# A decode step of two attention layers: VectorE takes seven of eight value chunks and also adds key blocks

## The chip, the core and the metric

The kernel runs on one NeuronCore of a Trainium2 chip. The metric is the device time of one execution in microseconds (us). Every input lies in the chip's main memory in float32 and is streamed into the on-chip memory (SBUF, 128 partitions) while TensorE (PE), VectorE (DVE), ScalarE (ACT) and GpSimd (POOL) compute. SyncE (SP) issues the loads. All of them read instructions in order, each from its own list, and wait for one another by semaphores.

## The reference

One token passes twice through the same attention layer A and the same MLP layer B. The cache of keys and values has 32 heads of 4096 positions of 128 numbers.

```python
def _A_ref(x, k_cache, v_cache, wq, wo):
    B, Sq, D = x.shape                                     # 1, 1, 512
    H, Dh = 32, 128
    q = (x @ wq).reshape(B, Sq, H, Dh).transpose(0, 2, 1, 3)
    scores = jnp.einsum("bhqd,bhkd->bhqk", q, k_cache) * (Dh ** -0.5)
    p = _softmax(scores, axis=-1)
    o = jnp.einsum("bhqk,bhkd->bhqd", p, v_cache)
    return o.transpose(0, 2, 1, 3).reshape(B, Sq, H * Dh) @ wo

def _B_ref(x, w1, b1, w2, b2):
    h = _gelu(jnp.einsum("bsd,df->bsf", x, w1) + b1)       # F = 1376
    return jnp.einsum("bsf,fd->bsd", h, w2) + b2

x = A_x
x = x + _A_ref(_layernorm(x, axis=-1), A_k_cache, A_v_cache, A_wq, A_wo)
x = x + _B_ref(_layernorm(x, axis=-1), B_w1, B_b1, B_w2, B_b2)
x = x + _A_ref(_layernorm(x, axis=-1), A_k_cache, A_v_cache, A_wq, A_wo)
x = x + _B_ref(_layernorm(x, axis=-1), B_w1, B_b1, B_w2, B_b2)
```

Keys and values together are far larger than SBUF, so each layer reads them again, apart from a little that is kept at the change of layers.

## The kernel before

**Tiles.** The 32 heads form G = 8 groups of J = 4. A group has one block K and one block V, each 128 partitions by 16,384 numbers, in C = 8 chunks of 2048 (NC). A chunk of V holds, for each of the four heads, 512 positions: 128 on the partitions, times four key blocks of 128 numbers each (U = 512 numbers per head). A third load of a group, the pair, brings the group's part of `wo` and the next group's part of `wq` (2 x 2048 numbers).

**Homes.** K and V go around three homes of one large tile, `arena`: A, B and C (`RING`). K of the group after next lies where V of this group lay. The pair has one home, `PAIR`. `SCRATCH`, `TURNED` and the rest have places behind them.

**Order of the loads.** All loads are issued by SP in the order of the program: K, V, pair, K, V, pair. A load waits until its home's last reader is done, and every later load waits behind it. Line 108 issues them all.

**One group.** `group` computes the scores, chunk by chunk into the PSUM tile `pS` (`scores`, four narrow products side by side, one per head). Between chunks it finishes the group before (`ahead`). Behind chunk 4 (`SUM_BEHIND`) `sum_up` adds what VectorE has made into the PSUM tile `pO`, and `head` (line 286 on) turns `pO`, picks out the blocks on the diagonal, and sums the four key blocks. Behind chunk 6 `out_product` multiplies with `wo`, and so frees the pair. Then come chunk 7, the softmax (`exponentials`, lines 230 to 239) and the turned weights (`weights`, lines 244 to 253). In the last group of layer two the output product stands behind chunk 7 instead.

**Values.** `partly` gives the first `by_pe` chunks of V to PE (`values`), which writes four rows per head, one per key block, of which the diagonal is wanted. `weighted` (line 264) multiplies the other chunks in place by the softmax weights, in one VectorE instruction over the whole remainder. Then `next_queries` forms the next group's queries on PE and VectorE, and `added` sums those chunks on VectorE by halves until one chunk is left. With `by_pe` = 2 there are six chunks: adds of three, one and one chunk. The sum over the 128 partitions is left to `sum_up`: four products of a column of ones with the chunk, one per head.

This way go groups 0 to 5 of layer one, and five groups of layer two, the first of them with `by_pe` = 3. The last two groups of layer one and the first two of layer two give all values to PE, around the change of layers.

**The end.** The last K comes in two halves, the last V in four pieces. Behind them come the last `wo`, `w1` and `w2`, which the MLP takes as they land.

**Order by hand.** `tc.keep_in_program_order` keeps PE's products, the loads, and the multiplications and adds of line 264 in the order in which the program names them. In the trace, products of every helper have line 112, and loads line 108.

Of the kernel before, what the change touches and what calls it, by code (L numbers as in the profile page):

```python
# [14 lines left out]
ALU = mybir.AluOpType  # L15
AX = mybir.AxisListType

P = 128
# [3 lines left out]
G = 8  # L22
J = 4
C = 8
# [4 lines left out]
U = 512  # L29
NC = 4 * U  # L30
# [9 lines left out]
SHARED = B_AT + KEPT_V  # L40
SCRATCH = SHARED + 10 * U
PAIR = SHARED + 11 * U
KEPT_K = PAIR + 2 * NC
TURNED = SHARED + 9 * U
ARENA = KEPT_K + 2 * U
HALVES = ((0, 4), (4, 8))
BY_PE, BY_PE_AT_BEGIN = 2, 3
SUM_BEHIND = 4
ZQ = C - 1 + J * C
WIDE = 32 * J + 8 + 3 + 1  # L50
FRONT = 192
# [8 lines left out]
def decode_layers(ctx: ExitStack, tc: tile.TileContext, vectors, k, v, w, w1, w2, out):  # L60
    nc = tc.nc
# [3 lines left out]
    def ctile(name, *shape):  # L65
        return const.tile([P, *shape], F32, name=name)
# [4 lines left out]
    front = ctile("front", FRONT)  # L71
    arena = const.tile([P, ARENA], F32, name="arena")
    cells = ctile("cells", CELLS)
# [9 lines left out]
    def small(name, n=1):  # L83
        nonlocal first_front, rest
        if name.startswith("gelu_"):
            i = "huaztg".index(name[-1])
            return cells[:, gelu + FB * i : gelu + FB * (i + 1)]
        if name not in places:
            fit = [j for j in range(J) if gaps[j] + n <= ends[j]]
            if name == "by_dma":  # L90
                places[name] = front, first_front, n
                first_front += n
            elif fit:
                places[name] = cells, gaps[fit[0]], n
                gaps[fit[0]] += n
            else:
                places[name] = cells, rest, n
                rest += n
        t, a, m = places[name]
        assert m == n and first_front <= FRONT and rest <= CELLS  # L100
        return t[:, a : a + n]

    def at(first, n):
        return arena[:, first : first + n]
# [6 lines left out]
    def matmul(*a, **kw):  # L111
        tc.keep_in_program_order(nc.tensor.matmul(*a, **kw))  # L112

    def quarters(first):
        return [at(first + U * j, U) for j in range(4)]
# [21 lines left out]
    power = small("power")  # L137
    nc.gpsimd.memset(power, -0.5)

    one = small("one")  # L140
    nc.vector.memset(one, 1.0)


    pS, pO = (psum.tile([P, 512], F32, name=n) for n in ("pS", "pO"))
# [7 lines left out]

    turned_at = [at(TURNED, P)]

# [6 lines left out]
    def pairs(t):  # L161
        return t[:, :8].rearrange("p (c i) -> p c i", i=2)
# [61 lines left out]
    def scores(z, c, kt):  # L224
        for j in range(J):
            matmul(pS[32 * j : 32 * j + C, :], z[:, C * j + C - 1 - c : C * j + 2 * C - 1 - c], kt[j],
                   start=(c == 0), stop=(c == C - 1))

    def exponentials(sc, nsc, between=None):
        nc.vector.tensor_reduce(ml[:, 0:1], pS, axis=AX.X, op=ALU.max)  # L230
        m, bias = small("m"), mt
        nc.vector.transpose(mt, ml)
        nc.vector.tensor_reduce(m, mt[:, :C], axis=AX.X, op=ALU.max)
        nc.vector.tensor_scalar(mb[:, :C], m.to_broadcast([P, C]), nsc, None, op0=ALU.mult)  # L234
        nc.vector.transpose(bias, mb)  # L235
        if between:
            between()
        p = at(SCRATCH, U)
        nc.scalar.activation(p, pS, AF.Exp, bias=bias[:, 0:1], scale=sc, accum_out=ml[:, 0:1])  # L239
        return p  # L240
# [12 lines left out]
        nc.vector.reciprocal(rl, lr[:, 0:1])  # L253
        return pt, rl

    def values(i, pt, vt, c):
        for j in range(J):
            matmul(pO[32 * j : 32 * j + 4, :], pt[:, c, j, :], vt[j],
                   start=(i == 0), stop=(i == C - 1))


# [1 line left out]
    def pinned(*a, **kw):  # L263
        tc.keep_in_program_order(nc.vector.tensor_tensor(*a, **kw))  # L264
# [6 lines left out]
    def added(home, by_pe=BY_PE):  # L271
        first, n = home + NC * by_pe, C - by_pe
        while n > 1:
            m = n // 2
            a, b = at(first + NC * (n - 2 * m), NC * m), at(first + NC * (n - m), NC * m)
            pinned(a, a, b, op=ALU.add)
            n -= m
        return quarters(first)

    def sum_up(t):  # L280
        for j in range(J):
            matmul(pO[32 * j : 32 * j + 4, :], one.to_broadcast([P, 4]), t[j], start=False, stop=True)

    def head(rl, last=False):
        ot = at(SCRATCH, U)
        nc.vector.transpose(ot, pO)  # L286
        o, on = small("o", 4), on_wide
        own = at(SCRATCH, 4 * 129).rearrange("p (b q) -> p b q", q=129)[:, :, :P]
        own = own.rearrange("p b (d q) -> p d b q", q=32)[:, :, :, 0]
        nc.vector.tensor_reduce(o, own, axis=AX.X, op=ALU.add)  # L290
        if last:
            nc.vector.tensor_scalar(on[:, :4], o, rl, None, op0=ALU.mult)  # L292
        else:
            nc.vector.tensor_scalar(in_quarters(on, 4), o.unsqueeze(1).to_broadcast([P, J, 4]), rl, None,
                                    op0=ALU.mult)
        return on
# [7 lines left out]
    def out_product(on, wt, to, narrow=False):  # L304
        for d in range(4):
            if narrow:
                for j in range(J):
                    matmul(to[32 * j : 32 * j + 1, :P], on[:, d : d + 1], wt[:, d, P * j : P * (j + 1)],
                           start=(d == 0), stop=(d == 3))
            else:  # L310
                matmul(to, on[:, d : d + P], wt[:, d, :], start=(d == 0), stop=(d == 3))
# [84 lines left out]
        return t  # L396


    def group(z, acc, ahead, k_blocks, out_behind=C - 2):
        for c, t in k_blocks:  # L400
            scores(z, c, t)
            if ahead and c == SUM_BEHIND:
                t, rl, wt = ahead
                sum_up(t)
                on = head(rl)
            if ahead and c == out_behind:
                out_product(on, wt, pO)
        p = exponentials(sc, nsc)
        if ahead:
            acc = add_up(acc, of_32(turned(pO, wide=True), 4))  # L410
        return acc, *weights(p)

    def partly(pt, v_blocks, home, by_pe=BY_PE):
        for c, t in v_blocks:
            if c < by_pe:
                values(c, pt, t, c)
        weighted(pt, home, by_pe)


    negm, z, sc, nsc = first_queries(xs, s, wq_t, wide=True)  # L420
    acc = pairs(xs)[:, :, 0]
    ahead = None
    for g in range(G):
        final = g == G - 1
        k_home, v_home = RING[2 * g % 3], RING[(2 * g + 1) % 3]
        acc, pt, rl = group(z, acc, ahead, blocks(k, g, k_home, HALVES if final else ((0, C),)))
        ahead = None
        if g == G - 2:
            nc.scalar.copy(at(KEPT_K, 2 * U), at(k_home + NC * C - 2 * U, 2 * U))
        if g < G - 2:  # L430
            partly(pt, blocks(v, g, v_home), v_home)
            pair = load(PAIR, of_w(g % 2, g, 2))
            z = next_queries(xs, negm, by_four(pair[:, NC:]), to=pS)
            ahead = added(v_home), rl, by_four(pair[:, :NC])
            continue
        for c, t in blocks(v, g, v_home, LAST if final else ((0, C),)):
# [3 lines left out]
            if g == G - 2:  # L440
                for j in range(J):
                    i = 4 * c + j - KEPT_V // U
# [8 lines left out]
        else:  # L451
            pair = load(PAIR, of_w(g % 2, g, 2))
            acc = add_up(acc, head_out(rl, by_four(pair[:, :NC])))
            wq_t = by_four(pair[:, NC:])
            z = next_queries(xs, negm, wq_t)
# [26 lines left out]
    negm, z, sc, nsc = first_queries(xs, s, wq_t)  # L482
    make_identity(nc, ident)
    acc = pairs(xs)[:, :, 0]
# [13 lines left out]
    p = exponentials(sc, nsc, lambda: queries(pO, negm, to=at(C_AT + 21 * U, P)))  # L498
    pt, rl = weights(p)
# [3 lines left out]
    acc = add_up(acc, of_32(turned(pO), 4))  # L503

    v_t = [at(B_AT + U * i, U) for i in range(KEPT_V // U)]
    for i, first in enumerate([SHARED, SHARED + U] + [PAIR + U * j for j in range(4)]):
        t = at(first, U)
# [4 lines left out]
    pt, rl = weights(exponentials(sc, nsc))  # L512
    for c in range(C):
        values(c, pt, v_t[4 * c : 4 * c + 4], c)
    acc = add_up(acc, head_out(rl, by_four(pair[:, NC:])))
    z = next_queries(xs, negm, by_four(pair[:, :NC]))

    turned_at[0] = at(TURNED, P)
    homes, ahead = (A_AT, C_AT, B_AT), None
    for n in range(2, G):  # L520
        g, final = G - 1 - n, n == G - 1
        k_home, v_home = homes[(2 * n - 1) % 3], homes[2 * n % 3]
        acc, pt, rl = group(z, acc, ahead, blocks(k, g, k_home, HALVES if final else ((0, C),)),
                            C - 1 if final else C - 2)
        if not final:
            by_pe = BY_PE_AT_BEGIN if n == 2 else BY_PE
            partly(pt, blocks(v, g, v_home, ((0, 6), (6, 8)) if n == 2 else ((0, C),)), v_home, by_pe)
            pair = load(PAIR, of_w(g % 2, g - 1, 2))
            z = next_queries(xs, negm, by_four(pair[:, :NC]), to=pS)
            ahead = added(v_home, by_pe), rl, by_four(pair[:, NC:])  # L530
            continue
        for c, t in blocks(v, g, v_home, LAST):
            values(c, pt, t, c)
            if c in (5, 7):
                idle(pS)
        wo_t = by_four(load(PAIR, of_w(g % 2, g, 1)))
        for a, b in W1_AT_END:
            load_w1(A_AT, a, b)
        for a, b in W2_AT_END:
            load_w2(A_AT + 11 * U, a, b)  # L540
        own = head_out(rl, wo_t, last=True)
# [46 lines left out]
```

## Time and profile before

| what | value |
|---|---|
| median of 3 runs | 673.24 us (672.96 to 673.5) |
| span of the profiled execution | 670.3 us |
| read from main memory | 285.62 MB, 426 GB/s over the span |
| mean granted clock of TensorE | 0.793 |
| matmuls of the scores (K chunks) | 145.2 us busy, 174.9 idle before, most of it for K |
| values on PE (pO from arena) | 81.7 us busy |
| VectorE, line 264 | 260.7 us busy |

The span goes from the first instruction to the last; the timed run holds some 3 us more around it. A row of the timeline gives start, duration, engine, line, operation and tiles, how many instructions were merged, and in square brackets the idle time before it and who ended it. A row of the windows gives for each engine its busy time and number of instructions, then the granted TensorE clock, the DMA share and the rate in GB/s. SPq is SyncE issuing a load.

### The profile page before, as it was taken

How to read it: one execution, taken by the hardware profiler on the slowest of the kernel's cores; microseconds unless marked ns; L12 is line 12 of the kernel's file. 1: busy time of each engine (PE TensorE's matmuls, PEld its weight loads, DVE VectorE, ACT ScalarE, POOL GpSimd, SP SyncE). 2: the span in 40 equal slices, each digit the busy share in tenths (PEclk: the TensorE clock that was granted, in tenths of full speed). 3: DMA queues.
4: the chain of work that ended last, by engine and by line, in shares of the span. 5: the costliest groups of instructions: out<-in, count | busy, mean ns of one | idle time of the engine just before them, and what ended most of it. 6: DMA issues, size and time to landing. Idle time of an engine off the chain costs nothing. (4 is left out here: it accounts for less than half of the span.)

```text
span 670.3 us, 5537 instructions
## 1 busy us (share of the span) xinstructions
PE 384.4 (57%) x2342; PEld 109.2 (16%) x2342; DVE 372.6 (56%) x480; ACT 22.8 (3%) x48; POOL 4.8 (1%) x23
## 2 busy tenths in 40 slices
PE   3533842636618546286768878737617456074586
PEld 1101210101102101021214222111102112011122
DVE  2059388395793965932112221392893966938822
ACT  0010000000000000002000110000000000000000
POOL 1000000000000000000000000000000000000000
PEclk9567785877678658778979998977669868687789
DMA  9999999999999999999999999999999999999996
GB/s 376 438 439 438 434 438 438 405 464 435 438 430 408 430 438 439 438 438 421 426 416 402 431 452 423 437 440 431 426 434 416 457 439 438 435 423 407 438 420 286
DMA packets 11256, 285.97 MB, mean 427 GB/s; under 512 B 1504, under 2 KB 1504, under 8 KB 3296
## 3 DMA queue, kind: packets, MB, share of 16 engines
q1 hardware_dynamic: 11088, 285.61, 99.1%
q8 instruction: 18, 0.29, 0.2%
q14 instruction: 6, 0.05, 0.0%
q10 hardware_dynamic: 144, 0.01, 0.0%
HBM read 285.62 MB, written 0.00 MB: 426 GB/s over the span
## 5 line engine op out<-in xcount | busy, mean ns | idle before, releaser
L264 DVE TENSOR_TENSOR arena<-arena 128x2048 f32<-128x2048 f32 (+4 forms) x44 | 260.7, 5924 | 16.6 <-DMA arena<-in_v 15.9
L112 PE MATMUL pS<-arena,front 128*8 128x512 f32 x1036 | 152.0, 713 | 174.9 <-DMA arena<-in_k 164.5
L112 PE MATMUL pO<-arena 128*4 128x512 f32 x504 | 81.7, 800 | 26.1 <-DMA arena<-in_v 24.5
L112 PE MATMUL pO<-arena,cells 128*128 128x512 f32 (+4 forms) x376 | 82.7, 506 | 17.2 <-POOL cells L186 6.7
L112 PEld LDWEIGHTS pS<-arena,front 128*8 128x8 f32 x1036 | 30.6, 102 | 289.1 <-DVE arena L264 141.9
L286 DVE STREAM_TRANSPOSE arena<-pO 128x512 f32<-128x512 f32 x16 | 11.5, 717 | 110.1 <-PE pO L112 110.1
L112 PE MATMUL pS<-arena,cells 128*1 128x128 f32 (+1 forms) x328 | 55.8, 385 | 18.5 <-DMA arena<-in_w 15.8
L170 DVE STREAM_TRANSPOSE arena<-pO 32x128 f32<-32x128 f32 x64 | 20.0, 312 | 59.0 <-PE pO L112 58.4
L112 PEld LDWEIGHTS pO<-arena,cells 128*128 128x128 f32 (+3 forms) x376 | 28.7, 122 | 64.7 <-issue 35.8
L230 DVE TENSOR_REDUCE cells<-pS 128x1 f32<-128x512 f32 x16 | 11.1, 692 | 50.1 <-PE pS L112 49.8
L244 PE MATMUL pO<-front,arena 128*128 128x128 f32 x64 | 12.0, 318 | 46.2 <-ACT arena L239 46.2
L112 PEld LDWEIGHTS pS<-arena,cells 128*1 128x1 f32 (+1 forms) x328 | 23.9, 120 | 61.2 <-issue 52.8
L239 ACT ACTIVATE arena<-pS,cells 128x512 f32<-128x512 f32 x16 | 12.4, 777 | 507.1 <-DVE cells L235 507.1
L112 PEld LDWEIGHTS pO<-arena 128*4 128x4 f32 x504 | 13.5, 99 | 76.2 <-issue 66.3
L244 PEld LDWEIGHTS pO<-front,arena 128*128 128x128 f32 x64 | 7.6, 154 | 60.2 <-ACT arena L239 59.1
L170 DVE STREAM_TRANSPOSE arena<-pS 32x128 f32<-32x128 f32 x44 | 13.7, 312 | 1.6
L249 DVE STREAM_TRANSPOSE cells<-cells 128x32 f32<-128x32 f32 x16 | 3.4, 214 | 15.9 <-ACT arena L239 15.7
L390 DVE MEMSET pS<- 128x512 f32 x11 | 5.3, 485 | 1.2
L174 DVE STREAM_TRANSPOSE arena<-pS 128x128 f32<-128x128 f32 x3 | 1.0, 317 | 8.9 <-PE pS L112 8.9
L199 DVE TENSOR_SCALAR cells<-cells,pS 128x4 f32<-128x4 f32 x4 | 0.9, 234 | 7.9 <-PE pS L112 7.9
L112 PE MATMUL pO<-arena,front 128*128 128x128 f32 (+2 forms) x18 | 5.1, 382 | 0.0
L247 DVE COPY arena<-pO 128x128 f32<-128x128 f32 x16 | 4.2, 261 | 0.7 <-PE pO L244 0.5
(62 smaller groups left out, 72.5 us busy)
## 6 DMA issues: line engine op xcount, KB each, us to landing
arena<-in_w SPq DMA_DIRECT2D x13, 2048.0 KB, 11.2
arena<-in_k SPq DMA_DIRECT2D x4, 4096.0 KB, 24.9
arena<-in_v SPq DMA_DIRECT2D x2, 4096.0 KB, 38.7
arena<-in_w SPq DMA_DIRECT2D x6, 1024.0 KB, 21.1
arena<-in_v SPq DMA_DIRECT2D x3, 2048.0 KB, 42.5
arena<-in_v SPq DMA_DIRECT2D x1, 6144.0 KB, 30.2
arena<-in_w SPq DMA_DIRECT2D x6, 688.0 KB, 25.9
arena<-in_v SPq DMA_DIRECT2D x4, 1024.0 KB, 46.0
```

Source lines behind the costliest of these rows:

```text
L112: tc.keep_in_program_order(nc.tensor.matmul(*a, **kw))
L170: turn = nc.vector.transpose(t[q], src[q, P * j : P * (j + 1)])
L174: nc.vector.transpose(t, src[:, :P])
L199: nc.vector.tensor_scalar(xc, pairs(xs)[:, :, 0], nm, None, op0=ALU.add)
L230: nc.vector.tensor_reduce(ml[:, 0:1], pS, axis=AX.X, op=ALU.max)
L239: nc.scalar.activation(p, pS, AF.Exp, bias=bias[:, 0:1], scale=sc, accum_out=ml[:, 0:1])
L244: tc.keep_in_program_order(nc.tensor.transpose(pT[:, b].rearrange("p j r -> p (j r)"), p[:, P * b : P * (b + 1)], ident))
L247: nc.vector.tensor_copy(pt, pT[:, :, :, :C].rearrange("p b j c -> p c j b"))
L249: nc.vector.transpose(lt, ml)
L264: tc.keep_in_program_order(nc.vector.tensor_tensor(*a, **kw))
L286: nc.vector.transpose(ot, pO)
L390: nc.vector.memset(pS, 0.0)
```

## The change

`by_pe` becomes 1 for nine of the eleven groups, so VectorE multiplies seven chunks there. In the first such group of layer two it becomes 2 (from 3), and in the last 3 (from 2). `added` goes two steps further: after the chunks it adds key blocks 2 and 3 to 0 and 1, and then 1 to 0, so one block of 128 numbers per head is left. Its sum over partitions is one product instead of four: the weights are a mask `PICK`, 128 columns with ones at columns 0, 33, 66 and 99, so head j's sum is added to row 32 j + j of `pO`, and the block on the diagonal is right, while nothing is added elsewhere. Since that product adds to all 128 rows, PE's own values now write all 32 rows of each head (`rows=32`). The mask is set by two GpSimd memsets in each layer. The sum stands behind chunk 5 instead of 4, and in the last group behind chunk 3, between the two halves of K, with the output product behind chunk 6 there as elsewhere.

```diff
-BY_PE, BY_PE_AT_BEGIN = 2, 3
-SUM_BEHIND = 4
+PICK = SHARED + 8 * U
+BY_PE, BY_PE_AT_BEGIN, BY_PE_AT_END = 1, 2, 3
+SUM_BEHIND, SUM_BEHIND_AT_END = 5, 3
...
-    one = small("one")
-    nc.vector.memset(one, 1.0)
...
-    def values(i, pt, vt, c):
+    def values(i, pt, vt, c, rows=4):
+        w = pt.rearrange("p c j b -> p (c j b)")
         for j in range(J):
-            matmul(pO[32 * j : 32 * j + 4, :], pt[:, c, j, :], vt[j],
+            first = 4 * (J * c + j)
+            matmul(pO[32 * j : 32 * j + rows, :], w[:, first : first + rows], vt[j],
                    start=(i == 0), stop=(i == C - 1))
...
             pinned(a, a, b, op=ALU.add)
             n -= m
-        return quarters(first)
+        t = at(first, NC).rearrange("p (j b d) -> p j b d", j=J, b=4)
+        for n in (2, 1):
+            pinned(t[:, :, :n], t[:, :, :n], t[:, :, n : 2 * n], op=ALU.add)
+        return t[:, :, 0]
+
+    def set_pick():
+
+        t = at(PICK, 33 * J)
+        nc.gpsimd.memset(t, 0.0)
+        nc.gpsimd.memset(t.rearrange("p (j q) -> p j q", j=J)[:, :, 0], 1.0)
 
     def sum_up(t):
-        for j in range(J):
-            matmul(pO[32 * j : 32 * j + 4, :], one.to_broadcast([P, 4]), t[j], start=False, stop=True)
+        matmul(pO.rearrange("p (j d) -> p j d", j=J), at(PICK, P), t, start=False, stop=True)
...
-    def group(z, acc, ahead, k_blocks, out_behind=C - 2):
+    def group(z, acc, ahead, k_blocks, sum_behind=SUM_BEHIND):
         for c, t in k_blocks:
             scores(z, c, t)
-            if ahead and c == SUM_BEHIND:
+            if ahead and c == sum_behind:
                 t, rl, wt = ahead
                 sum_up(t)
                 on = head(rl)
-            if ahead and c == out_behind:
+            if ahead and c == C - 2:
                 out_product(on, wt, pO)
...
             if c < by_pe:
-                values(c, pt, t, c)
+                values(c, pt, t, c, rows=32)
...
         acc, pt, rl = group(z, acc, ahead, blocks(k, g, k_home, HALVES if final else ((0, C),)),
-                            C - 1 if final else C - 2)
+                            SUM_BEHIND_AT_END if final else SUM_BEHIND)
         if not final:
-            by_pe = BY_PE_AT_BEGIN if n == 2 else BY_PE
+            by_pe = {2: BY_PE_AT_BEGIN, G - 2: BY_PE_AT_END}.get(n, BY_PE)
```

`set_pick()` is called once ahead of layer one's groups and once ahead of layer two's loop.

More of the change, by code (lines that the diff above doesn't have):

```diff
@@ L421, in decode_layers @@
     acc = pairs(xs)[:, :, 0]
+    set_pick()
     ahead = None
@@ L518, in decode_layers @@
     turned_at[0] = at(TURNED, P)
+    set_pick()
     homes, ahead = (A_AT, C_AT, B_AT), None
```

## The prediction

> **What bounds the kernel now.** I read the page's first lines, then the windows by stage.
>
> ```profile
> span 670.3 us, 5537 instructions
> PE 384.4 (57%) x2342; PEld 109.2 (16%) x2342; DVE 372.6 (56%) x480; ACT 22.8 (3%) x48; POOL 4.8 (1%) x23
> DMA  9999999999999999999999999999999999999996
> ```
>
> ```profile
> 350.00:380.00 30.00, 25.39 (x324) 10.59 (x321) 7.88 (x39) 1.84 (x5) 2.16 (x8) 1.00 1.02 413
> 100.00:300.00 200.00, 101.92 (x502) 27.69 (x503) 140.06 (x129) 4.52 (x9) 0.00 (x0) 0.74 1.00 433
> 640.00:664.00 24.00, 19.61 (x149) 5.82 (x147) 6.79 (x32) 1.08 (x3) 0.85 (x3) 0.93 1.00 422
> ```
>
> The DMA line is full and every engine idles much. In the long stage the DMA share is 1.00 and the rate 433 GB/s (last two columns); the change of layers (350 to 380) and the end lose a little, and the change edits neither. So less work on PE or VectorE shortens nothing by itself. The change can only matter where it makes the stream run dry, or behind the last load. Who lets the next loads go? The DMA queue's own waits, then one group of layer one in the timeline (K2 is the block whose scores start at 113.44; all below is counted from that row):
>
> ```profile
> SPq L108 <- PE pO L112: 382.5, 16, 33.0
> ```
>
> ```profile
> 69.99 6.98 PE L112 MATMUL pS<-arena,front 128*8 128x512 f32 x40 [13.94 <-DMA arena<-in_k]
> 89.26 12.96 DVE L264 TENSOR_TENSOR arena<-arena 128x12288 f32<-128x12288 f32 x1 [0.96 <-DMA arena<-in_v]
> 103.98 0.48 DVE L390 MEMSET pS<- 128x512 f32 x1
> 104.38 11.20 DVE L264 TENSOR_TENSOR arena<-arena 128x6144 f32<-128x6144 f32 x3
> 113.44 5.75 PE L112 MATMUL pS<-arena,front 128*8 128x512 f32 x40 [15.62 <-DMA arena<-in_k]
> 119.01 1.04 PE L112 MATMUL pO<-arena,cells 128*4 128x512 f32 x8
> 119.86 1.90 PE L112 MATMUL pS<-arena,front 128*8 128x512 f32 x16
> 121.69 3.70 PE L112 MATMUL pO<-arena,cells 128*128 128x512 f32 x8
> 125.42 0.33 SPq L108 DMA_DIRECT2D arena<-in_w  x1
> 126.75 0.69 DVE L230 TENSOR_REDUCE cells<-pS 128x1 f32<-128x512 f32 x1
> 132.73 12.96 DVE L264 TENSOR_TENSOR arena<-arena 128x12288 f32<-128x12288 f32 x1 [2.02 <-DMA arena<-in_v]
> ```
>
> The queue waits for PE's pO: the next w pair goes out only when the output product (121.69) has read the old pair, and the next K and V stand behind it. Only V is then left in flight; it lands 19.3 after K (132.73). So the issue at K+12.0 has slack. How much, the start says:
>
> ```profile
> 0.74 0.37 SPq L108 DMA_DIRECT2D arena<-in_w  x1
> 0.74:1.73 0.99, 0.00 (x0) 0.00 (x0) 0.79 (x5) 0.00 (x0) 0.53 (x3) 1.00 0.00 0
> 1.73:2.73 1.00, 0.00 (x0) 0.00 (x0) 0.58 (x3) 0.00 (x0) 0.00 (x0) 1.00 1.02 164
> ```
>
> A load moves nothing for 1.0 us after its issue. **The pair must be out by K+18.3**, so the slack is 6.3 us.
>
> **The loop that the change lengthens.** The summing product (119.01) starts the chain: 6.4 us to the pair's issue, 11.7 to the point at which VectorE could start the next multiplication (132.73 less its 2.02 idle, 130.71). Multiplication, queries and adds run from 89.26 to 115.58: 26.3. Together 38.0, while K comes every 43.45 (69.99 to 113.44): 5.4 to spare, so VectorE waits for V and each group begins afresh. Now the new durations:
>
> ```profile
> L264 DVE TENSOR_TENSOR arena<-arena 128x12288 f32<-128x12288 f32 x10 | 129.6, 12958 | 15.9 <-DMA arena<-in_v 15.9
> L264 DVE TENSOR_TENSOR arena<-arena 128x6144 f32<-128x6144 f32 x10 | 65.4, 6542 | 0.0
> L264 DVE TENSOR_TENSOR arena<-arena 128x2048 f32<-128x2048 f32 x22 | 50.4, 2292 | 0.8
> L264 DVE TENSOR_TENSOR arena<-arena 128x10240 f32<-128x10240 f32 x1 | 10.8, 10826 | 0.0
> L264 DVE TENSOR_TENSOR arena<-arena 128x4096 f32<-128x4096 f32 x1 | 4.4, 4408 | 0.0
> ```
>
> - Seven chunks multiplied: 2048 more elements cost 12.96 - 10.83 = 2.13, so 15.09.
> - Adds of seven chunks: 6.54 + 4.41 + 2.29 (three, two, one chunk). Then two new adds over key blocks, 1024 and 512 elements. The trace has none so short or strided: at least 0, at most 2.29 each, the 2048 row. By the slope (1.04 per 1024, 0.18 fixed) 1.23 and 0.71; I take these, nearest to the row's own size. With gaps 15.3.
> - Queries and memset between them: 102.22 to 104.38, 2.16, unchanged.
>
> That makes 15.1 + 2.2 + 15.3 = **32.6 instead of 26.3**. The masked product stays at about 0.9: one 128-column product is a quarter of the output product's 3.70, and the four narrow ones took 0.85 together. Its wider weights cost 0 to 0.2 more; I take 0. The loop is then 11.7 + 32.6 + 0.1 for the hand-over = 44.4, and **0.9 longer than K's 43.45**. The cover is gone: from the second full group on VectorE no longer waits for V but for PE, and the delay is handed on and grows.
>
> PE loses one chunk of values (0.86 at full clock) in nine groups, one in the first of layer two and gains one in the group before the last. It comes before the next queries, which VectorE takes only after its multiplication, so it hides: 0. The wider weight loads for it (32 rows) hide behind products. Two small POOL memsets per layer, on an engine 1% busy, lie well ahead of their first reader: 0.
>
> **Does the stall also cost clock?** PE now stands still behind its sixth chunk until the adds end. Four adjoining windows of 3.41 us, between steps of the granted clock (the third column from the right):
>
> ```profile
> 228.68:232.10 3.42, 1.59 (x4) 0.38 (x2) 3.42 (x1) 0.00 (x0) 0.00 (x0) 1.00 0.88 383
> 232.10:235.51 3.41, 0.00 (x0) 0.00 (x0) 3.12 (x8) 0.00 (x0) 0.00 (x0) 1.00 1.20 519
> ...
> 440.31:443.72 3.41, 1.32 (x4) 0.25 (x2) 3.41 (x1) 0.00 (x0) 0.00 (x0) 1.00 0.89 384
> 443.72:447.14 3.42, 0.00 (x0) 0.00 (x0) 3.13 (x8) 0.00 (x0) 0.00 (x0) 0.50 1.06 460
> ```
>
> With 1.59 busy of 3.42 the next window keeps full clock, with 1.32 of 3.41 it drops to 0.50. A stall of about 2.1 us inside one window is enough. At half clock the output product's 3.7 takes 7.4; lower bound of the surcharge 0, upper 3.7 a group. The windows' phase is not tied to the work, so a stall of 2 to 6 us is caught in some groups, in part: I take a third, 1.2, from K3 on. The Trainium skill ("TensorE: Matmul & The Clock Gate", Part 1 and "HAM oscillation") describes the same free-running windows of 3413 ns, but lets the clock fall after a whole idle window, so that only idle gaps above some 3.4 us hurt; the row at 440.31 speaks against that, and by its rule the clock would hold through stalls of 2 and 3 us, which gives the first rival's time.
>
> **Group by group, layer one.** Adds end for K2 at 89.26 + 32.6 = 121.9, so its sum starts at K+8.5; its six chunks are ready at 119.9, a stall of 2.0. Issue K+14.9.
> - K3: sum 8.5 + 0.9 = 9.4; issue 9.4 + 6.4 + 1.2 = 17.0, in time.
> - K4: sum 9.4 + 0.9 + 1.2 = 11.5; issue 19.1, late by 0.8.
> - K5: 11.5 + 2.1 - 0.8 = 12.8; issue 20.4, late by 2.1.
> - K6: the same, 2.1.
>
> DMA stands still 0.8 + 2.1 + 2.1 = **5.0 us**. At the change of layers PE is late but the last V of layer one is queued; I count nothing more.
>
> **Layer two** has fewer such groups, and its first has six chunks only.
>
> ```profile
> 475.81 12.96 DVE L264 TENSOR_TENSOR arena<-arena 128x12288 f32<-128x12288 f32 x1 [1.39 <-DMA arena<-in_v]
> 499.97 7.03 PE L112 MATMUL pS<-arena,front 128*8 128x512 f32 x40 [13.63 <-DMA arena<-in_k]
> ```
>
> 475.81 + 32.6 = 508.4 is K+8.4 of the block at 499.97. The two blocks behind it: 9.3 with issue 16.9; 11.4 with issue 19.0, late by **0.7**.
>
> **The end.** Here nothing absorbs a delay:
>
> ```profile
> 630.70 1.20 PE L112 MATMUL pS<-arena,front 128*8 128x512 f32 x8 [3.88 <-DMA arena<-in_k]
> 632.95 1.89 PE L112 MATMUL pO<-arena,cells 128*4 128x512 f32 x8 [1.05 <-DVE arena L264]
> 634.61 4.58 PE L112 MATMUL pS<-arena,front 128*8 128x512 f32 x24
> 639.12 3.70 PE L112 MATMUL pO<-arena,cells 128*128 128x512 f32 x8
> 646.34 6.39 PE L112 MATMUL pO<-arena 128*4 128x512 f32 x48 [0.39 <-DVE arena L247]
> 664.24 1.93 PE L112 MATMUL pS<-arena,cells 128*1 128x128 f32 x64 [1.16 <-DVE cells L339]
> ```
>
> ```profile
> 647.61 18.66 DMA arena<-in_w
> ...
> 666.32 0.62 PE pS L112 x16
> ```
>
> PE ends its eight w2 chunks at 666.17, the last load lands at 666.27: 0.1 of slack. Before, the values start 15.6 after the last half of K (630.70 to 646.34). After: weights ready in the group before at 11.4 + 11.7 + 1.2 = K+24.3; five chunks cost 10.83 + 2.16 + (4.41 + 2.29 + 2.29 + 1.23 + 0.71 + 0.1 gaps) = 24.0; adds end K+48.3, which is 4.2 after the last half of K (43.45 + 0.7 behind). Then, at the rows' half clock: sum 1.7, three chunks 4.5, the output product, which now stands ahead of the last chunk, 3.7, that chunk 0.9, softmax 4.0 (126.75 to 130.71): 14.8, so 19.0. Later by 3.4; a full clock there would give back up to 2.7 (0.86 a chunk and 0.85 for the sum); I take 0.8, since the stall ahead of the sum leaves the clock low for a window at least. Less the slack of 0.1: **2.5**.
>
> Sum: 5.0 + 0.7 + 2.5 = 8.2. The profiled execution has a span of 670.3, and the median of the runs is 673.24, 2.9 above it; I add to each: 678.5 span, **681.4 us** forecast.
>
> **Rivals.**
> - **The clock holds** (full clock at each stall, by luck of the phase or because 2 us are too short). Sums at 8.5, 9.4, 10.3, 11.2, 12.1, issues to K+18.5: 0.2 late in all. The end: weights ready at 10.2 + 11.7, adds at K+45.9, 2.4 behind the last K against 2.25; later by up to 1.5, given back by full clock. Time 672.9 to 674.9, say 673.6. It decides if the surcharge stays under 0.3 a group. For it: windows with 1.59 busy held. Against: from K3 on the stall is 3 us and more (9.4 less the 6.4 at which six chunks end), near a whole window.
> - **The loop stays shorter than the stream**: VectorE's addition 1 us cheaper than summed, for instance new adds at almost nothing. Then each group waits for V as now, the issue is at K+14.5 at most, and nothing is lost: 673.2. The point is 43.45 - 11.8 = 31.7 for VectorE's part. Against: the five rows lie on one line.
> - **Dearer strided adds**, 2.29 each: the loop is 47.0, K2 issues at 17.5, and each later group is some 3.5 late: about 13 in layer one, 6 in layer two, 4 at the end: 696.
> - **Faster**: full clock and an earlier sum save time ahead of the last values. But the last load lands as before, with 0.1 of slack: 673.0; for more than 1.35 the stream would have to quicken, which no row promises.
>
> **How the numbers follow.** Forecast case 66% (675 to 688), the clock holds 14%, the shorter loop 9%, dearer adds 5%, faster 6%. About 0.2% (1.35 us) is what a measurement tells from no change: slower 71%, within 23%, faster 6%. The range 673.0 to 687.0 leaves out most of the faster case, the dear adds and the forecast's far edge; the forecast's own is 675 to 688.
>
> **What would show it.** Right: adds of L264 some 15 us, and sums of pO waiting for DVE arena (only 1.05 us in all now) for 2 to 5 us from the third group on; SPq issues of the pair 17 to 21 after K; slots of DMA under 9 before 300 us; half clock inside the output product. Wrong: if VectorE still waits for DMA arena<-in_v ahead of every multiplication (15.9 in all now), the loop is not closed; if it waits for PE yet the pair is out by K+18, the clock held. If the stream is full and the span longer, the end alone is to blame.

## The result, and the profile after

| | before | changed |
|---|---|---|
| median of the timed runs | 673.37 us (672.96 to 673.5) | 678.25 us (677.52 to 679.87) |
| ratio to before, 95% interval | | 1.0081 (1.0065 to 1.0097) |
| span of the profiled execution | 670.3 us | 678.1 us |

The changed kernel is slower by 4.9 us. Its profiled execution is the longest of its four (679.87 us), so its span shows 7.8 us more, 2.9 us above what the medians differ by. Medians, ratios and ranges here and below leave out the two runs that fell into a slower state of the chip (one of the sum behind chunk 4, one of the pair in two loads). Lines have moved by one: products now have line 113, loads 109, VectorE's multiplications and adds 265.

The page of the changed kernel, its first two parts and the chain that ended last:

```profile
span 678.1 us, 5284 instructions
PE 393.2 (58%) x2204; PEld 115.5 (17%) x2204; DVE 432.8 (64%) x501; ACT 22.8 (3%) x48; POOL 5.3 (1%) x27
...
DMA  9999999999999999999999999999999999999996
...
DVE 22%; PE 12%; DMA 7%; issue 1%; ACT 1%; DVEq 0%; ACTq 0%
```

VectorE is busy 60 us longer. The DMA row looks as full as before: slices of 17 us hide gaps of one. The chain has changed: it began with "DMA 28%; PE 13%" before, and is led by VectorE now.

The groups of VectorE's line 265, kept apart by shape:

```profile
L265 DVE TENSOR_TENSOR arena<-arena 128x14336 f32<-128x14336 f32 x9 | 135.8, 15092 | 6.3 <-DMA arena<-in_v 6.3
L265 DVE TENSOR_TENSOR arena<-arena 128x4096 f32<-128x4096 f32 x10 | 44.2, 4422 | 0.3
L265 DVE TENSOR_TENSOR arena<-arena 128x1024 f32<-128x1024 f32 x11 | 13.5, 1224 | 0.4
```

The seven-chunk multiplication takes the 15.09 us forecast, and the strided add 1.22 against 1.23. In the last column, all waits for V ahead of multiplications have shrunk from 15.9 to 6.3 us.

The timeline of the changed kernel, VectorE, PE and the queue put together, from the second multiplication of layer one to the fourth:

```profile
89.48 15.09 DVE L265 TENSOR_TENSOR arena<-arena 128x14336 f32<-128x14336 f32 x1 [0.76 <-DMA arena<-in_v]
...
106.73 15.31 DVE L265 TENSOR_TENSOR arena<-arena 128x6144 f32<-128x6144 f32 x5
...
113.66 7.70 PE L113 MATMUL pS<-arena,front 128*8 128x512 f32 x48 [13.83 <-DMA arena<-in_k]
122.09 1.13 PE L113 MATMUL pO<-arena 128*128 128x512 f32 x2 [0.74 <-DVE arena L265]
...
124.51 3.70 PE L113 MATMUL pO<-arena,cells 128*128 128x512 f32 x8 [0.32 <-DVE cells L303]
128.24 0.33 SPq L109 DMA_DIRECT2D arena<-in_w  x1
...
133.72 15.09 DVE L265 TENSOR_TENSOR arena<-arena 128x14336 f32<-128x14336 f32 x1
...
177.95 15.09 DVE L265 TENSOR_TENSOR arena<-arena 128x14336 f32<-128x14336 f32 x1
```

The multiplication at 89.48 still waited for V, those at 133.72 and 177.95 have no idle time before them. From one to the next is 44.24 and 44.23 us: that is the loop, forecast at 44.4, against K's 43.45. The sum now waits for VectorE (122.09), and the pair goes out at 128.24, 14.6 us after K, where it was 12.0.

Windows of the changed kernel, each from one K to the next. The first number behind the two ends is the length, the last is the rate:

```profile
113.66:157.31 43.65, 22.89 (x94) 6.42 (x95) 36.60 (x31) 0.87 (x2) 0.00 (x0) 0.73 1.00 427
157.31:201.20 43.89, 21.56 (x94) 5.89 (x95) 36.81 (x32) 0.87 (x2) 0.00 (x0) 0.77 1.01 436
201.20:246.72 45.52, 23.51 (x94) 6.60 (x95) 37.19 (x32) 0.87 (x2) 0.00 (x0) 0.72 1.00 429
246.72:291.12 44.40, 23.05 (x94) 6.55 (x95) 37.32 (x32) 0.98 (x3) 0.00 (x0) 0.73 0.99 421
```

The same four windows before:

```profile
113.44:156.93 43.49, 21.09 (x109) 5.73 (x110) 31.05 (x30) 0.87 (x2) 0.00 (x0) 0.74 1.00 434
156.93:200.42 43.49, 22.90 (x108) 6.33 (x109) 30.93 (x30) 0.87 (x2) 0.00 (x0) 0.74 1.01 434
200.42:243.87 43.45, 23.79 (x109) 6.58 (x110) 30.84 (x30) 0.87 (x2) 0.00 (x0) 0.74 1.01 435
243.87:287.65 43.78, 21.81 (x108) 5.81 (x109) 30.89 (x30) 0.98 (x3) 0.00 (x0) 0.77 1.00 432
```

The first group (43.65) lies within what before shows, the other three are longer: 177.5 us for the four instead of 174.2. Length times rate says how much was moved: 76.0 MB instead of 75.6. At the former rate those 76.0 MB take some 175.2 us, so only about 2.3 of the 3.3 us are lost by the stream itself. In the rest K lands later than its share of the bytes.

Where K lands, compared row by row with before: K2 of layer one is 0.2 us late, and K6 starts at 291.12 against 287.65, 3.5 us late. The block of layer two that started at 499.97 starts at 506.71, 6.7 late, so K6's own pair and the change of layers added 3.3. From there to the last but one K nothing is added (594.01 against 587.33), and the rest of the span adds 1.1.

### The profile page after: what moved, and what is told of

Read it like the earlier page. It is cut to its first block, busy times and chain, and to the rows that moved or that the text cites. A ratio compares the mean times of both kernels' runs of the same rounds, so it can differ in the third digit from the quotient of the medians.

```text
span 678.1 us, 5284 instructions
## 1 busy us (share of the span) xinstructions
PE 393.2 (58%) x2204; PEld 115.5 (17%) x2204; DVE 432.8 (64%) x501; ACT 22.8 (3%) x48; POOL 5.3 (1%) x27
## 5 line engine op out<-in xcount | busy, mean ns | idle before, releaser
L265 DVE TENSOR_TENSOR arena<-arena 128x1024 f32<-128x1024 f32 (+5 forms) x66 | 320.1, 4850 | 8.9 <-DMA arena<-in_v 6.3
L113 PE MATMUL pO<-arena 128*4 128x512 f32 (+2 forms) x454 | 82.3, 780 | 30.5 <-DVE arena L265 16.2
L113 PE MATMUL pO<-arena,cells 128*128 128x512 f32 (+3 forms) x288 | 72.3, 474 | 19.1 <-POOL arena L288 6.7
L113 PE MATMUL pS<-arena,cells 128*1 128x128 f32 (+1 forms) x328 | 66.1, 420 | 26.6 <-DMA arena<-in_w 24.0
L295 DVE STREAM_TRANSPOSE arena<-pO 128x512 f32<-128x512 f32 x16 | 11.5, 717 | 63.7 <-PE pO L113 63.7
L243 PE MATMUL pO<-front,arena 128*128 128x128 f32 x64 | 15.7, 392 | 47.1 <-ACT arena L238 47.1
L113 PEld LDWEIGHTS pS<-arena,cells 128*1 128x1 f32 (+1 forms) x328 | 28.1, 133 | 76.5 <-issue 67.9
L113 PEld LDWEIGHTS pO<-arena,cells 128*128 128x128 f32 (+2 forms) x288 | 27.0, 134 | 60.7 <-issue 29.8
L113 PEld LDWEIGHTS pO<-arena 128*4 128x4 f32 (+2 forms) x454 | 15.2, 113 | 79.9 <-issue 41.5
L243 PEld LDWEIGHTS pO<-front,arena 128*128 128x128 f32 x64 | 10.0, 194 | 61.3 <-ACT arena L238 60.1
L248 DVE STREAM_TRANSPOSE cells<-cells 128x32 f32<-128x32 f32 x16 | 3.4, 214 | 16.7 <-ACT arena L238 16.7
```

The costliest lines, as they stand in the source:

```text
L243: tc.keep_in_program_order(nc.tensor.transpose(pT[:, b].rearrange("p j r -> p (j r)"), p[:, P * b : P * (b + 1)], ident))
L248: nc.vector.transpose(lt, ml)
```

## The experiments

All were timed beside runs of the kernel before on the same chip, whose median lay between 672.3 and 672.7 us there. The ratios are the surer comparison with the changed kernel's 1.0081, for several kernels scatter by some us from run to run.

| kernel | median, us | lowest to highest | ratio to before (95%) |
|---|---|---|---|
| six chunks again | 673.20 | 672.2 to 674.7 | 1.0005 (0.9996 to 1.0015) |
| no key blocks | 673.47 | 672.1 to 674.3 | 1.0010 (1.0001 to 1.0019) |
| sum behind chunk 4 | 679.17 | 678.5 to 682.6 | 1.0106 (1.0075 to 1.0137) |
| before, padded by 4.4 us | 672.46 | 672.1 to 674.2 | 0.9998 (0.9988 to 1.0007) |
| before, padded by 6.5 us | 687.27 | 682.7 to 691.0 | 1.0218 (1.0162 to 1.0274) |
| pair in two loads | 679.48 | 674.4 to 680.5 | 1.0072 (1.0043 to 1.0102) |
| light last group | 679.86 | 676.4 to 680.3 | 1.0098 (1.0073 to 1.0123) |
| both of these | 675.87 | 674.1 to 680.8 | 1.0050 (1.0030 to 1.0070) |
| before, pair late, two products | 684.40 | 680.1 to 686.1 | 1.0169 (1.0123 to 1.0215) |
| before, pair late, four products | 692.80 | 691.0 to 693.8 | 1.0297 (1.0277 to 1.0317) |
| stall filled | 680.33 | 679.0 to 683.1 | 1.0120 (1.0095 to 1.0145) |
| PE takes five chunks at the end | 679.32 | 673.7 to 682.6 | 1.0097 (1.0065 to 1.0130) |

### Is it the length of VectorE's part?

The changed kernel with six chunks:

```diff
-BY_PE, BY_PE_AT_BEGIN, BY_PE_AT_END = 1, 2, 3
+BY_PE, BY_PE_AT_BEGIN, BY_PE_AT_END = 2, 2, 3
```

> The changed kernel, but VectorE takes six chunks again (two stay with PE) in the nine groups; key blocks are still added, the mask and the later sum stay. Loop theory: VectorE's part is 12.96 + 2.16 + 11.2 + 2.0 = 28.3 us, with 11.8 around it 40.1, under the 43.45 between two K's, so each group waits for V again and the time is that of before, 673.3 (672.5 to 674.3). Rival, that the place of the sum, the wide rows or the masked product costs: it stays near 678.

Measured 673.20, no different from before. The mask, the wide rows, the key blocks and the new places are all in it, so none of them costs by itself where the loop has slack (at most 1.0 us by the interval).

With seven chunks, but the old summing:

```diff
-        t = at(first, NC).rearrange("p (j b d) -> p j b d", j=J, b=4)
-        for n in (2, 1):
-            pinned(t[:, :, :n], t[:, :, :n], t[:, :, n : 2 * n], op=ALU.add)
-        return t[:, :, 0]
+        return quarters(first)
...
-        matmul(pO.rearrange("p (j d) -> p j d", j=J), at(PICK, P), t, start=False, stop=True)
+        for j in range(J):
+            matmul(pO[32 * j : 32 * j + 4, :], one.to_broadcast([P, 4]), t[j], start=False, stop=True)
...
-                values(c, pt, t, c, rows=32)
+                values(c, pt, t, c)
```

> The changed kernel with seven chunks, but without the adds over key blocks and the mask: four narrow products with ones again, four rows of values. Loop theory: VectorE's part is 15.09 + 2.16 + 13.4 = 30.7 us, the loop 42.4, 1 us under 43.45, so nothing is lost: 673.5 (672.7 to 675). Rival, that the seventh chunk by itself is what costs: 676 or more.

Measured 673.47: at most 1.3 us of loss by its interval, most likely 0.7. The seventh chunk alone fits; only chunk and key blocks together do not. Its groups of line 267 still wait for V:

```profile
L267 DVE TENSOR_TENSOR arena<-arena 128x14336 f32<-128x14336 f32 x9 | 135.8, 15093 | 10.6 <-DMA arena<-in_v 10.5
```

The sum behind chunk 4:

```diff
-SUM_BEHIND, SUM_BEHIND_AT_END = 5, 3
+SUM_BEHIND, SUM_BEHIND_AT_END = 4, 3
```

> The changed kernel with the sum behind chunk 4 as before. Loop theory: PE waits for the adds at either place, so 678.2 within 1 us. Rival, that the later place of the sum costs: some 0.9 us a group back, 673 to 675.

Measured 679.17, within the 1 us that was expected, and the interval holds the changed kernel's ratio. No gain, so the later place is not the cost.

Then the length alone, with nothing else of the change: an instruction that changes no value, added to the kernel before (two chunks, and three in a second kernel; the last group of layer two is spared).

```diff
-    def added(home, by_pe=BY_PE):
+    def added(home, by_pe=BY_PE, more=True):
         first, n = home + NC * by_pe, C - by_pe
+        if more:
+            again = at(first, NC * 2)
+            pinned(again, again, again, op=ALU.max)
...
-            ahead = added(v_home, by_pe), rl, by_four(pair[:, NC:])
+            ahead = added(v_home, by_pe, n < G - 2), rl, by_four(pair[:, NC:])
```

> The kernel before, with one idle VectorE instruction more ahead of the adds in every group but the last (the maximum of two chunks with themselves, 4096 elements, 4.4 us). Loop 38.0 + 4.4 = 42.4, under 43.45: nothing lost, 673.2 (672.4 to 674.2). If every us on VectorE costs something: 675 or more.

> The same with three chunks, 6144 elements, 6.54 us, about what the change adds. Loop 44.6, 1.1 over K's 43.45, with none of the change in it. Loop theory: five sums of layer one drift by 1.1 each, and it is as slow as the changed kernel, 678 to 682. If the change's own products, mask or places cost, it stays near 673 to 675.

Measured 672.46 and 687.27. That is the knee the loop asks for: 4.4 us more on VectorE in ten groups cost nothing, 6.5 us cost 14.6 us in all. The mechanism holds; the size was missed (678 to 682 expected). In layer one the multiplications of the padded kernel follow one another at 44.43 us (89.28 to 133.71), as they should. In layer two the trace shows what goes with the greater loss, PE's rows in the last block but one:

```profile
595.42 6.19 PE L112 MATMUL pS<-arena,front 128*8 128x512 f32 x40 [13.76 <-DMA arena<-in_k]
606.92 1.89 PE L112 MATMUL pO<-arena,cells 128*4 128x512 f32 x8 [5.31 <-DVE arena L264]
608.59 3.64 PE L112 MATMUL pS<-arena,front 128*8 128x512 f32 x16
612.15 3.89 PE L112 MATMUL pO<-arena,cells 128*128 128x512 f32 x8
```

After a stall of 5.31 us the sum (1.89 instead of 1.04) and two chunks (3.64 instead of 1.90) ran at half clock, and the output product starts 5.2 after the sum instead of 2.7. Up to this block 8.1 us are lost (595.42 against 587.33), and 6.5 more from it to the end of the span.

### Is the loss paid where the pair goes out late?

The changed kernel with the pair in two loads, the queries' half first (layer one shown):

```diff
-            pair = load(PAIR, of_w(g % 2, g, 2))
-            z = next_queries(xs, negm, by_four(pair[:, NC:]), to=pS)
-            ahead = added(v_home), rl, by_four(pair[:, :NC])
+            wq_t = by_four(load(PAIR + NC, of_w(g % 2, g + 1, 1)))
+            wo_t = by_four(load(PAIR, of_w(g % 2, g, 1)))
+            z = next_queries(xs, negm, wq_t, to=pS)
+            ahead = added(v_home), rl, wo_t
```

> The changed kernel, but each pair is loaded as two loads of 1 MB, the queries' half first, which need not wait for the output product. Nothing of the loop is changed; when K lands, 2.4 us more of transfers stand behind V. If the loop costs through the late issue of the pair, most of the loss comes back: 674 to 676. If it costs otherwise (VectorE or PE in the way of the transfers, or the delay of PE itself): 678 and above.

Measured 679.48: missed on the median, and no gain that is clear of the noise. But its runs fall apart: five took 677.9 to 680.5 us, and two took 674.4, which is what was expected if the late pair is all. The profiled execution is the longest of these seven, and in it the stream did what it should in layer one. Windows from K to K, then PE's rows around the last sum of layer one, in this kernel:

```profile
113.52:157.05 43.53, 23.05 (x94) 6.45 (x95) 36.65 (x31) 0.87 (x2) 0.00 (x0) 0.74 1.01 434
157.05:200.59 43.54, 23.46 (x95) 6.42 (x95) 36.76 (x32) 0.87 (x2) 0.00 (x0) 0.74 1.00 434
200.59:244.60 44.01, 23.61 (x94) 6.72 (x95) 35.73 (x32) 0.87 (x2) 0.00 (x0) 0.73 1.01 437
244.60:288.02 43.42, 20.81 (x95) 5.65 (x96) 35.46 (x32) 0.98 (x3) 0.00 (x0) 0.78 1.00 428
```

```profile
288.02 7.66 PE L113 MATMUL pS<-arena,front 128*8 128x512 f32 x48 [15.61 <-DMA arena<-in_k]
300.30 2.07 PE L113 MATMUL pO<-arena 128*128 128x512 f32 x2 [4.63 <-DVE arena L265]
```

Four groups take 174.5 us instead of the changed kernel's 177.5 (the 174.2 of before), so K6 starts 3.1 us earlier than in the changed kernel. But the sum that waits for VectorE comes at 300.30, and in the changed kernel it came at 300.30 too: the loop is as long as ever. In this execution the next steps lose what the stream no longer loses at the pairs: from K6 to the block of layer two that started at 456.53 before it takes 175.6 us, where the changed kernel takes 172.1 and the kernel before 168.9.

So lateness carried to the end of layer one was tried next. In its last group on VectorE PE takes three chunks, as the change itself does at the end of layer two:

```diff
-            partly(pt, blocks(v, g, v_home), v_home)
+            by_pe = BY_PE_AT_END if g == G - 3 else BY_PE
+            partly(pt, blocks(v, g, v_home), v_home, by_pe)
...
-            ahead = added(v_home), rl, by_four(pair[:, :NC])
+            ahead = added(v_home, by_pe), rl, by_four(pair[:, :NC])
```

> The changed kernel, but in the last group of layer one that uses VectorE PE takes three chunks (as the change does at the end of layer two), so VectorE's part is 24 us there and no delay is carried into the change of layers. Theory now, after the split pair left the sums where they were: the loop's lateness (5.4 us at the end of layer one) is paid in full, partly where the stream runs thin, the rest at the change of layers, which waits for compute. Then about 2 us come back: 676.3 (675.3 to 677.5). Rival, that only the stream's thin places at the pairs cost: 678.2.

> Both together: pairs in two loads and the light last group. With lateness paid at either place: the first edit keeps the stream full, the second drops what was late before the change of layers, so layer one loses about 0.5 us and the time is 674.5 (673.5 to 676.2). If lateness is not what is paid, or the split itself costs: 678 or above, as for the split alone.

Alone 679.86: missed. Together 675.87, inside the expected range: by the medians neither edit gains by itself, and both together return 2.4 us of the changed kernel's 4.9 (678.25 to 675.87; by ratios 0.0031, with intervals that just overlap). Against the light group alone the gain is clear. Against the split pair alone it is not (1.0050 lies inside its interval, 1.0043 to 1.0102), so that it takes both edits is not shown by the times. The traces bear it out in one execution each: with the split pair in both, the light group shortens the way from K6 over the change of layers from 175.6 to 172.0 us. That fits a lateness which is paid at whichever place next has no slack.

The profiled execution of the light group alone shows its gain and where it went. It starts the block of layer two at 504.07, 2.6 us ahead of the changed kernel (506.71). The block behind that takes 45.63 us instead of 43.78: there the sum runs at half clock (1.93 instead of 1.13, behind a stall of 2.72), and the pair goes out at K+16.8 instead of K+15.6. At the last K but one 0.8 us of the gain are left (593.20 against 594.01).

### How late may the pair be?

The kernel before, with two products added (four in a second kernel) where PE would stand still anyway; they read the pair and so hold it:

```diff
+        if ahead and out_behind == C - 2:
+            for _ in range(2):
+                idle(pK[0], of=PAIR)
         p = exponentials(sc, nsc)
```

> The kernel before, with two idle products more behind the eighth chunk of scores in every group but the last; they read the pair, so its successor is issued later, at about K+14.6 to K+16.2 instead of 12.0 to 13.6, while PE would stand still there anyway: the loop keeps its 38 us. By the prediction's deadline (K+18.3, when V has landed, less 1.0) nothing is lost: 673. By the changed kernel's trace (DMA engines end their share of V over some 3 us, and the first of them stand still): 0.3 to 0.8 in each of ten groups, 676 to 680.

> The same with four idle products, issue at K+16.3 to K+17.9, loop longer by 0.5 at most. By the prediction's deadline still nothing: 673 to 674. By the spread of the engines: 1 to 2 us in each of ten groups, 683 to 693.

Measured 684.40 and 692.80: 12.1 and 20.5 us above before, more than expected for the first and near the top for the second. The prediction's deadline falls. With four products, the queue's row of one group, the window to the next K, and VectorE's multiplications:

```profile
131.92 0.33 SPq L108 DMA_DIRECT2D arena<-in_w  x1
```

```profile
114.12:159.84 45.72, 26.82 (x116) 8.25 (x117) 31.57 (x30) 0.87 (x2) 0.00 (x0) 0.76 0.97 413
```

```profile
L264 DVE TENSOR_TENSOR arena<-arena 128x12288 f32<-128x12288 f32 x10 | 129.6, 12958 | 17.0 <-DMA arena<-in_v 17.0
```

The pair is out at K+17.8, inside the K+18.3 that was thought safe, and the group is 2.3 us longer than 43.45. VectorE still waits for V as before (17.0 in all), so its loop has nothing to do with it. With two products the same views show the pair out at K+15.4, and three groups of 43.95, 44.28 and 45.28 us:

```profile
130.64 0.33 SPq L108 DMA_DIRECT2D arena<-in_w  x1
```

```profile
115.22:159.17 43.95, 23.73 (x112) 6.94 (x113) 29.57 (x30) 0.87 (x2) 0.00 (x0) 0.77 0.97 413
159.17:203.45 44.28, 23.84 (x112) 6.95 (x113) 30.93 (x30) 0.87 (x2) 0.00 (x0) 0.77 1.00 425
203.45:248.73 45.28, 24.62 (x112) 7.39 (x113) 32.25 (x30) 0.87 (x2) 0.00 (x0) 0.76 1.02 430
```

So issues at K+14.9 to K+15.8, those of the kernel with two products, cost 1.2 us a group on the mean (12.1 over ten), and issues at K+16.7 to K+18.2, with four, cost 2.0 (20.5 over ten). Up to K+14.2 nothing is lost: with six chunks an issue at K+14.16 has a block of 43.46 us. Around K+15 there is no sharp edge. In the changed kernel an issue at K+15.5 goes with 44.40 us (layer one) and one at K+15.6 with 43.78 (layer two), which before has too.

The packets in the trace show how a pair can be late though V has not landed. Sixteen are in flight at a time, as many as there are DMA engines. At the changed kernel's issue of 217.96, K+16.8, V's packets were already running out: at 218.5 nine were in flight. V's last sixteen packets ended over 2.1 us there, and over 1.6 to 3.4 in the other groups that were read. V "lands" with the last of them; engines that are done stand still earlier.

### Does the clock take its part, and the end?

The changed kernel with its stall filled, so that the granted clock stays up:

```diff
                 t, rl, wt = ahead
+                for _ in range(2):
+                    idle(pK[0], of=SCRATCH)
                 sum_up(t)
```

> The changed kernel, with two idle products (1.7 us) ahead of the sum, where PE stands still for the adds, so that the granted clock does not fall. If the half clock at the stall makes the difference between its runs and costs, on the mean, 1 to 2 us: 676.5 to 677.5 with less spread. If the clock holds there anyway: 678.2. As the prediction had it (1.2 us in each of six groups): 673 to 675.

Measured 680.33, and PE at full clock in the group where the changed kernel had been slow. First the changed kernel, then this one:

```profile
210.56 2.04 PE L113 MATMUL pO<-arena 128*128 128x512 f32 x2 [2.76 <-DVE arena L265]
212.53 1.77 PE L113 MATMUL pS<-arena,front 128*8 128x512 f32 x8
214.23 3.70 PE L113 MATMUL pO<-arena,cells 128*128 128x512 f32 x8
```

```profile
210.95 1.02 PE L113 MATMUL pO<-arena 128*128 128x512 f32 x2
211.90 1.05 PE L113 MATMUL pS<-arena,front 128*8 128x512 f32 x8
213.26 3.70 PE L113 MATMUL pO<-arena,cells 128*128 128x512 f32 x8 [0.32 <-DVE cells L303]
```

None of the loss returns, so the half clock at the sum is not what the changed kernel pays for on the whole. The filling products may delay a sum by up to about half a us themselves, so this bounds the clock's share and does not measure it.

PE taking five chunks in the last group on VectorE:

```diff
-BY_PE, BY_PE_AT_BEGIN, BY_PE_AT_END = 1, 2, 3
+BY_PE, BY_PE_AT_BEGIN, BY_PE_AT_END = 1, 2, 5
```

> The changed kernel, but PE takes five chunks in the last group that uses VectorE, whose part is then 15.4 us; the sum between K's halves no longer waits. If the end costs 2.5 us, as predicted: 675.7. If the end keeps step with the late stream, as the trace looks: 678 within 1 us.

Measured 679.32, with seven runs from 673.7 to 682.6: no gain. A return of 2.5 us would be a ratio of about 1.004, below the interval (1.0065 to 1.0130), so the end does not cost 2.5 us.

## Why the prediction was right, and where it was wrong

**Right: what bounds, and the loop.** That less work on PE would not shorten the kernel, that VectorE's part would be 32.6 us and the loop close over K's period, and that each group would then be late, all came as worked out. VectorE's part measures 122.04 - 89.48 = 32.56 (89.48 is the multiplication, 106.73 + 15.31 the end of the adds). The first sums, K+8.4 at 122.09 and in layer two, were forecast at K+8.5 and K+8.4. One reading behind it was slightly off: the slope of the five rows is 1.07 us per 1024 elements (12.96 less 2.29 over 10,240), not 1.04. The times taken from it, 1.23 and 0.71, hold all the same: 1.22 and 0.69 were measured. The knee was tested from both sides: six chunks, or seven without key blocks, or a pad of 4.4 us cost nothing that matters; a pad of 6.5 us, without any of the change, does.

What followed from the closed loop came otherwise. All times count from the block's K:

| block | sum, forecast | sum, measured | pair out, forecast | pair out, measured |
|---|---|---|---|---|
| K2 | 8.5 | 8.4 | 14.9 | 14.6 |
| K3 | 9.4 | 9.0 | 17.0 | 15.2 |
| K4 | 11.5 | 9.4 | 19.1 | 16.8 |
| K5 | 12.8 | 9.3 | 20.4 | 15.5 |
| K6 | 12.8 | 9.2 | 20.4 | 15.3 |

No pair went out later than K+16.8, so by the prediction's own deadline layer one would have lost nothing.

**Wrong: the deadline of the pair, K+18.3.** It took V's landing, less the 1.0 us in which a load moves nothing. The packets confirm the 1.0 us (0.94 to 1.0 from issue to first packet wherever engines stood still), but V's landing is that of the slowest engine. Loss begins somewhere between K+14.2 and K+15.5, and it grows gradually and unevenly from there, instead of 1:1 from K+18.3. K3 with its pair at K+15.2, priced at 0, may already have lost some 0.4 (43.89 against 43.45); for K2 at K+14.6 no loss shows (43.65, where before reaches 43.78). Since K loses time in each block, the sums stay within 1 us of the first one's place behind K, instead of 4.3 us behind it at K6 as forecast.

**Wrong: the surcharge of 1.2 us a group for half clock.** The output product took 3.70 in every group of the changed kernel. One sum and one chunk ran slow, 2.04 and 1.77 instead of 1.12 and 1.05: 1.6 us once in layer one, where 4.8 were priced. The stalls were 0.7 to 2.8 us instead of 2 to 6, for two reasons. A thin stream makes K late too and so shortens PE's wait for VectorE. And the six chunks took 6.6 to 8.1 us (7.70 at 113.66), where the prediction took 6.4 from a single block: that block's five chunks, 5.75 us, were the quickest of layer one, where others took 6.2 to 7.4. Where a stall did reach 5.3 us, in the padded kernel, the half clock came. Behind the 4.15 us of the last block it came later: the sum still took 1.13, and the 24 score products behind it 4.46 us, where eight at full clock take 1.05.

These two errors work against each other. Up to K6 the prediction had 0.8 + 2.1 = 2.9, and the trace shows 3.3 from K2 on; K6's pair and the change of layers had 2.1 and show 3.3. That layer one's 5.0 us came near what the profiled execution lost there is luck. The change of layers was priced at nothing: that step was wrong too, as the profiled execution of the split pair shows, where lateness that the pairs no longer cost was lost there. How much is its own is not settled: in three kernels without drift (six chunks, no key blocks, pad of 4.4 us) the way from K6 to the block of layer two took 168.9, 169.8 and 170.3 us.

**The signs that were named.** Sums that wait for VectorE came (16.2 us in all, where it was 1.05), but for 0.7 to 2.8 us in layer one, not 2 to 5. Pairs out at K+17 to K+21, slots of DMA under 9 and half clock inside the output product did not come. And pairs out by K+18, which were to mean that the clock held and little was lost, came together with the loss.

**Wrong in size: the end, 2.5 us.** The mechanism was a late sum ahead of the last values, with 0.1 us of slack. The sum did come late, and the first values too:

```profile
639.59 1.13 PE L113 MATMUL pO<-arena 128*128 128x512 f32 x2 [4.15 <-DVE arena L265]
653.84 7.03 PE L113 MATMUL pO<-arena 128*4 128x512 f32 x48 [0.42 <-DVE arena L246]
672.37 2.75 PE L113 MATMUL pS<-arena,cells 128*1 128x128 f32 x88 [1.15 <-DVE cells L348]
```

The values start 7.5 us later than before (653.84 against 646.34), but the stream is 7 to 8 us late by then as well. All eleven w2 chunks run in one piece, for the last load is there in time, and from their start to the end of the span it is 5.7 us (678.1 less 672.37) against 6.1 before (670.3 less 664.24). The 3.4 us of extra lateness rested on two surcharges of 1.2 and on a sum at K+11.4 in the group before; that sum came at K+9.9 (603.89 behind 594.01). The light end (five chunks) gained nothing. Together with the 0.7 of the last pair, 3.2 us were priced and 1.1 came.

So the sum of 8.2 us stands against 7.8 in the profiled execution, which is the long one, and 4.9 in the median. The sign was right, and so was the loop as the cause. The path from the loop to the time was right in kind, late pairs, but not in its deadline, its surcharge and its end; that these add up to nearly the profiled loss is luck. The median forecast is 3 us too late. Which terms were smaller in the runs around the median no trace shows, for only the longest was profiled.

**The rivals.** "The clock holds" was nearly right about the clock and wrong about the time (673.6), because it used the same deadline. "The loop stays shorter" is what the experiment without key blocks makes true, and 673.47 is what it gives, against the 673.2 of the rival. Dearer strided adds are excluded by the measured 1.22 and 0.69. The Trainium skill's rule ("TensorE: Matmul & The Clock Gate", "HAM oscillation") asks for no idle gaps above some 3.4 us. By it the six stalls of layer one, 0.3 to 2.8 us, would cost no clock, and that was nearly right here: only that of 2.76 us was followed by half clock, while 1.6 and less were not; the rows still show a drop well below 3.4.

## What to carry to other kernels

When a stream of loads is the bound, do not ask how busy an engine is, but how long the loop is that lets the next loads go, and compare it with the stream's own period: here a loop of 42.4 us (as worked out) against 43.45 cost nothing that matters, and 44.2 (as measured) cost 0.7%. Set the deadline of a load by the first DMA engine that runs out, not by the landing of the load ahead, which shows the last. And when one place where lateness is paid is mended, look for the next: both mended together gave back about half of the loss, and a shorter loop (six chunks) gave back all of it. Last, compare a forecast with the trace term by term: here the sum came close, while three of its terms did not.

## What had not been expected of the hardware

The last sixteen packets of one 8.4 MB load end over 1.6 to 3.4 us, so a successor that is issued some 3.9 us before the landing (around K+15.4 of 19.3) already costs about 1 us on the mean. The page's row of DMA busy time shows little of it. It stays at 9 in the changed kernel, and in the one with four late products, which lost 20 us, it reads:

```profile
DMA  9999999999898999998999999999998998998996
```
